# Attention products in 64-row tiles with the rounded part above the remainder, and new work lists, in a gated S4D and Infini-attention kernel

## The chip, the cores and the metric

The kernel runs on one core of a Trainium2 chip. Its time is the device time of one execution in microseconds (us); before the change three runs took 835.3, 832.37 and 835.19 us, median 835.19. PE is TensorE (the matrix engine), PEld its weight loads, DVE is VectorE, ACT is ScalarE, POOL is GpSimd, SP is SyncE, which here only issues transfers. Transfers are issued from SP's, ACT's and POOL's queues, each in order.

## What is computed

The input u has 2048 rows of 448 values. Two mixers work on it, and a gate per row joins them:

```python
g = sigmoid((u * gate_w).sum(-1))
out = g * A(u) + (1 - g) * B(u)
```

A is a long convolution along the rows: for each of 448 channels a kernel K of length 2048 is a sum over 256 complex exponentials, and y = irfft(rfft(u) * rfft(K)) + u * D_skip, with transforms of length 4096.

B is attention with memory: q, k and v are projections of u (16 heads of 28), the rows are cut into 4 segments of 512. In each segment and head:

```python
p = softmax(q @ k.T * scale + causal_mask)
o = sig(beta) * (phi(q) @ M) / (phi(q) @ z) + (1 - sig(beta)) * (p @ v)
M, z = M + phi(k).T @ v, z + phi(k).sum(0)
```

and the result is o @ wo. A softmax subtracts the largest logit of each row before the exponential.

## The kernel before

The program has two halves, one after the other on the same engines.

The first half builds the convolution kernel K. `first_half` (line 256 on) goes through 56 steps n: PE makes arguments (`turns`), ACT takes sines and cosines of them (`trig`), DVE multiplies them with decays (`product`), PE sums the products (`sums`), and POOL scales. Between these, at 190 places called slots, other work is fed in: `project` computes q, k, v, the memory and the gate, and `transform_u` the first Fourier step of u. The list FEED says how many steps of `project` go into each slot, FILL how many of `transform_u`, VECTOR at which slots the copies out of PSUM run on DVE instead of ACT, and UNREAD how many products without use (`k.turn_over`, 128 columns of bf16) stand ahead of each `sums`. The engines keep the order in which the program writes this. q and k are stored to DRAM (QD, KD) in two parts: `hi`, rounded to the type fp32r, and `lo`, the remainder. A weights' matrix, its rounded part and its remainder are treated likewise; `project` reads 128 rows of u at a time into `xin`, columns 384 to 447 twice (lines 922 and 923), since the last block of 64 columns is to fill 128.

The second half does the rest. `second_half` reads a list of words, PROGRAM, letter by letter; each letter issues one step:

- K: one of 8 steps of `transform_k`, the first Fourier step of K over its 64 x 112 sums; two PSUM tiles are copied out, one by ACT, one by DVE, and stored (GK).
- l: `load(i)`, q and k of the next of 16 units (a unit is one segment and 4 heads).
- A: one of 6 steps of `maxima(i)`: logits of two heads on PE, row maxima on DVE. The logits use the rounded parts alone.
- B: the end of a unit's maxima: a transpose, the negative maxima rounded and their remainder (`mn`), and a write of them into row 28 of q, from POOL's queue (line 1075). Since k has 1 in its row 28 and q and k have 28 values a head, the next product already gives the logit less the maximum.
- W: one of 6 steps of `weigh(i)`: transposed logits of two heads on PE, in three products (hi by hi, lo by hi, hi by lo), then the exponential on ACT; a seventh W issues POOL's masks. P is two W steps of one kind abreast.
- V: the weights times v. E: the end of a segment (division by the sums, the memory's part, the output projection).
- C: a step of `convolve`: second Fourier step of K and u in 64-row tiles, their product on POOL, the way back; its loads run three steps ahead. F, b, j, z: the last step of the convolution and the join with the gate. G, w, S, D: the gate, wo, the skip term, a division of the last segment.
- t: a product without use, 128 rows, 512 columns, bf16 (`turn_over`).

A head has 28 values in a tile of 32 rows, so four heads fill 128 partitions, and the products of A and W are issued in tiles of 32 rows of the array: A works on heads 2 and 3 where W works on heads 0 and 1, and the other way round (`MSTEPS`, line 1038). `PLACES` lists the blocks below the diagonal: 512 columns, then 384 and 128, then 256.

The tiles of q and k have 4 buffers each. Space and order of the transfers: `k.dma` issues from SP and is kept behind the last marked transfer (`k.mark`).

## Time and profile before

| | |
|---|---|
| runs (us) | 835.3, 832.37, 835.19 |
| the profiled execution, by the same clock (us) | 836.45 |
| its span in the trace (us) | 834.7 |
| busy: PE, DVE, ACT, POOL (us) | 727.2, 569.5, 555.2, 239.1 |
| granted PE clock, mean | 0.950 |
| moved by DMA | 153.99 MB, 184 GB/s on average |

The span is cut below at 66, 85, 436, 490 and 740 us from its start. Up to about 66 us the parameters are prepared, up to 436 us the loop of the first half runs, then the passage, in which the K steps and the first units stand, and from about 490 us attention and convolution go side by side; after 740 us the convolution's last step and the last segment remain. Busy times of PE count matmuls from issue to the modelled end of the pipeline, so they overlap and are no measure of throughput. "Granted clock" is the share of full speed that the throttle gave to PE.

### The profile page before, as it was taken

To read this page: it belongs to the slowest core of one execution; us is meant where nothing else is said; L and a number is where in the kernel's file an instruction comes from. 1 tells how busy PE (TensorE), PEld (TensorE's weight loads), DVE (VectorE), ACT (ScalarE), POOL (GpSimd) and SP (SyncE) were. 2 spreads that over 40 slices of the span, in tenths; PEclk is the share of its full clock that TensorE was granted. 3 is DMA by queue.
4 is the path that set the end of the run, shared out by engine and by line. 5 is a ranking of instruction groups with operands and counts; after the bars stand their busy time and mean duration, and the time that the engine had idled before them with its cause. 6 is when DMAs were issued, how large, how long until landed. Compare 5 with 4: busy or idle time off the path is not lost.

```text
span 834.7 us, 19015 instructions
## 1 busy us (share of the span) xinstructions
PE 727.2 (87%) x7557; PEld 398.3 (48%) x7582; DVE 569.5 (68%) x1134; ACT 555.2 (67%) x663; POOL 239.1 (29%) x249
## 2 busy tenths in 40 slices
PE   1576998999879999799979899999999899988977
PEld 1353555665546655456644454444444344444433
DVE  7969489857989579886785864544554545666773
ACT  3767789979999899988872266765466544641320
POOL 4404210111001111011110035564545545752210
PEclk9879999999999999999995889999999899999999
DMA  8527775145552455513647877685466565556775
GB/s 206 157 60 241 226 241 175 59 137 181 176 169 66 137 177 178 170 54 135 201 150 295 306 238 219 196 269 172 171 215 215 156 233 175 194 185 253 216 227 150
DMA packets 91987, 153.99 MB, mean 184 GB/s; under 512 B 23106, under 2 KB 60346, under 8 KB 91850
## 3 DMA queue, kind: packets, MB, share of 16 engines
q1 hardware_dynamic: 82826, 141.70, 53.2%
q10 hardware_dynamic: 7424, 9.18, 3.2%
q0 software_dynamic: 1648, 1.89, 0.8%
q8 instruction: 60, 0.98, 0.5%
q14 instruction: 29, 0.24, 0.1%
HBM read 91.74 MB, written 60.63 MB: 183 GB/s over the span
## 4 chain that ended last, share of the span: by engine, by line
PE 45%; DVE 18%; ACT 16%; DMA 9%; issue 7%; POOL 2%; SPq 1%; ACTq 0%; DVEq 0%; POOLq 0%
PE ps_m L1429 19%; PE ps_a L1429 18%; ACT cs L1394 7%; DVE Y L399 4%; DVE jk L1063 4%; PE ps_arg L1429 3%; PE ps_k L1429 3%; DVE X L395 2%; DVE Y L400 2%; ACT L1394 2%; PE ps_m L1432 1%; DMA r<-RD 1%; ACT EX L1394 1%; DMA bt<-BB 1%; DMA ce<-in_c_ce 1%
## 5 line engine op out<-in xcount | busy, mean ns | idle before, releaser
L1063 DVE CUSTOM_DVE_ANT_0 jk<-ps_a,mk 128x512 f32<-128x512 f32 (+3 forms) x256 | 125.1, 489 | 77.7 <-PE ps_a L1429 69.6
L361 POOL TENSOR_TENSOR EX<-EX,cab 128x1024 f32<-128x1024 f32 x28 | 53.5, 1913 | 301.7 <-ACT EX L1394 277.5
L1099 ACT ACTIVATE PT<-ps_a 128x1024 f32<-128x1024 f32 (+1 forms) x96 | 83.0, 880 | 69.6 <-PE ps_a L1429 68.6
L1394 ACT ACTIVATE cs<-ps_arg 128x1024 f32<-128x1024 f32 x111 | 107.4, 1023 | 1.4 <-DVE Y L400 0.8
L1429 PE MATMUL ps_a<-qu,ku 32*128 32x384 f32 (+3 forms) x768 | 78.3, 351 | 5.9 <-DVE mx L1063 5.0
L1429 PE MATMUL ps_m<-xh,w 128*128 128x512 f32 x224 | 81.8, 417 | 1.7 <-DMA w<-WD 1.4
L395 DVE TENSOR_TENSOR X<-EX,cs 128x1024 f32<-128x1024 f32 x56 | 69.2, 1236 | 17.8 <-ACT cs L1394 17.6
L663 POOL TENSOR_TENSOR pr<-us,ks 128x896 f32<-128x896 f32 x32 | 67.1, 2095 | 30.2 <-ACT us L662 30.1
L1110 POOL TENSOR_SCALAR_AFFINE_SELECT PT<-PT 128x256 f32<-128x256 f32 (+1 forms) x96 | 48.2, 507 | 93.3 <-ACT PT L1099 91.7
L1429 PE MATMUL ps_k<-Y,X 128*32 128x64 f32 x3584 | 62.2, 221 | 14.3 <-DVE Y L400 14.0
L1429 PEld LDWEIGHTS ps_k<-Y,X 128*32 128x32 f32 x3584 | 52.9, 110 | 39.1 <-DVE Y L400 27.0
L399 DVE TENSOR_TENSOR Y<-EY,cs 128x1024 f32<-128x1024 f32 x56 | 70.0, 1251 | 0.0
L1429 PEld LDWEIGHTS ps_a<-qu,ku 32*128 32x128 f32 x768 | 55.3, 193 | 20.2 <-DVE mx L1063 9.7
L1394 ACT ACTIVATE EY<-ps_arg 128x1024 f32<-128x1024 f32 x52 | 53.0, 1034 | 17.8 <-PE ps_arg L1429 16.4
L1394 ACT ACTIVATE cs<-cs 128x1024 f32<-128x1024 f32 x56 | 59.3, 1059 | 1.8
L401 DVE SCALAR_TENSOR_TENSOR Y<-EY,cs 128x512 f32<-128x512 f32 x56 | 40.9, 732 | 27.9 <-ACT cs L1394 25.8
L1429 PEld LDWEIGHTS ps_m<-xh,w 128*128 128x128 f32 x224 | 42.0, 187 | 21.9 <-issue 7.9
L1429 PE MATMUL ps_a<-ku,qu 32*128 32x512 f32 (+3 forms) x256 | 47.4, 404 | 4.5 <-DVE mx L1063 1.7
L1429 PE MATMUL ps_arg<-ct,lh 64*128 64x512 bf16 x224 | 45.5, 380 | 6.0 <-ACT cs L1394 4.3
L1429 PE MATMUL ps_m<-xl,w 128*128 128x512 f32 x128 | 50.2, 393 | 0.0
L1429 PEld LDWEIGHTS <-lh 64*128 64x128 bf16 x392 | 22.9, 95 | 55.2 <-issue 41.7
L1429 PEld LDWEIGHTS ps_a<-ku,qu 32*128 32x128 f32 x256 | 23.1, 195 | 48.2 <-issue 21.8
(215 smaller groups left out, 1429.4 us busy)
## 6 DMA issues: line engine op xcount, KB each, us to landing
w<-WD SPq DMA_DIRECT2D x32, 448.0 KB, 4.5
qu<-QD SPq DMA_DIRECT2D x16, 512.0 KB, 4.0
ku<-KD SPq DMA_DIRECT2D x16, 512.0 KB, 5.1
GU<-gs SPq DMA_DIRECT2D x32, 224.0 KB, 2.4
GK<-gs SPq DMA_DIRECT2D x8, 896.0 KB, 4.7
gk<-GK SPq DMA_DIRECT2D x32, 224.0 KB, 3.8
gu<-GU SPq DMA_DIRECT2D x32, 224.0 KB, 2.5
BB<-bs ACTq DMA_DIRECT2D x16, 448.0 KB, 4.5
```

Of the source, the lines that this page charges most:

```text
L361: nc.gpsimd.tensor_tensor(o, o, cab, ALU.mult)
L395: v.tensor_tensor(X, ex, t[:, :, 0], ALU.mult)
L399: v.tensor_tensor(Y[:, :, :, :32], lo, y[:, :, :, ::-1], ALU.mult)
L400: v.tensor_tensor(Y[:, 0, :, 32:], ey[:, :, 32:], y[:, 0], ALU.mult)
L401: v.scalar_tensor_tensor(Y[:, 1, :, 32:], ey[:, :, 32:], -1.0, y[:, 1], ALU.mult, ALU.mult)
L663: nc.gpsimd.tensor_tensor(pr[c], us, ks.pop(c), ALU.mult)
L1063: v.tensor_tensor_reduce(junk[:, :n], pt[:, x, o : o + n], k.mk[:, SEG - n :], 1.0, -3e38, ALU.add, ALU.max, mx[:, 3 - t, h : h + 1],)
L1099: nc.scalar.activation(PT[:, 2 * hp : 2 * hp + 2, 512 * b : 512 * b + n], pt[:, :, :n], AF.Exp, scale=SCALE)
L1110: nc.gpsimd.affine_select(sl, sl, pat, ALU.is_ge, 0.0, base=0, channel_multiplier=-1)
L1394: x = op(*args, **kw)
L1429: tc.keep_in_program_order(nc.tensor.matmul(*args, **kw))
L1432: tc.keep_in_program_order(nc.tensor.transpose(*args))
```

## The change

1. **q and k in 64-row tiles.** A unit's q now lies with heads in two row halves of 64: in each, 32 rows of the rounded part above 32 rows of the remainder; the other two heads lie beside them in a free dimension. k lies in the same rows twice, over both parts. One product over 64 rows then gives hi and lo of q at once against hi of k, and a second one against lo of k: two products where there were three (the product of the two remainders comes in as well). A's logits use both parts of q against hi of k, in one product as before. Both A and W use all 128 rows for two heads. P and `k.abreast` are gone, and each W step is on its own.
2. **Loads.** Eight transfers a unit instead of two, with k's bytes loaded twice; three buffers instead of four for q and for k. Unit 0's go over POOL's queue. The first two tiles of weights and the first of v are placed before the loads. The write of the negative maxima is four transfers instead of one, `mn` has one buffer instead of two, and `gs` of `transform_k` three instead of four.
3. **First half.** The second read of u's last columns becomes a copy on POOL; gate_w is loaded over POOL's queue. FEED, UNREAD, VECTOR and FILL have new numbers: UNREAD's sum goes from 24 to 94, VECTOR's from 66 to 78, FILL's from 9 to 10; FEED's stays 249.
4. **Words.** A new PROGRAM: t goes from 141 to 196 letters, a new letter T (two products without use in the two 64-row tiles) stands 17 times, P (9) is gone and W goes from 94 to 112; one K step (k) has both copies on ACT.

```diff
@@ -459,21 +459,21 @@
 FEED = (
-    2, 0, 3, 0, 1, 0, 2, 0, 1, 3, 8, 0, 0,
...
+    2, 0, 3, 0, 1, 0, 3, 0, 0, 3, 8, 0, 0,
...
@@ -491,30 +491,30 @@
 UNREAD = (
...
-    0, 0, 0, 0, 0, 0, 0, 0, 0, 0, 0, 16, 0, 8,
+    0, 0, 0, 0, 0, 0, 0, 0, 0, 8, 0, 0, 0, 0,
+    0, 0, 0, 16, 0, 0, 0, 0, 0, 0, 0, 4, 0, 0,
+    0, 0, 0, 0, 0, 0, 4, 0, 0, 0, 0, 0, 0, 20,
+    8, 0, 0, 0, 0, 0, 0, 2, 0, 0, 0, 16, 8, 8,
 )
...
@@ -600,7 +600,7 @@
     for i in range(8):
-        gs = fp.tile([128, 4, 4, 112], F32, tag="gs", name="gs", bufs=4)
+        gs = fp.tile([128, 4, 4, 112], F32, tag="gs", name="gs", bufs=3)
@@ -613,7 +613,7 @@
             pt = pts[jj][:, :, :448].rearrange("p j (n q) -> p j n q", n=4)
-            if jj == 0:
+            if jj == 0 or k.scalar_only:
@@ -739,9 +739,9 @@
     nc.gpsimd.memset(gw, 0.0)
-    nc.sync.dma_start(gw[:, :3, 0], k.gate_w[:384].rearrange("(k p) -> p k", p=128))
+    k.pdma(gw[:, :3, 0], k.gate_w[:384].rearrange("(k p) -> p k", p=128))
     for h in range(2):
-        nc.sync.dma_start(gw[64 * h : 64 * h + 64, 3, 0], k.gate_w[384:])
+        k.pdma(gw[64 * h : 64 * h + 64, 3, 0], k.gate_w[384:])
@@ -920,7 +920,7 @@
                 nc.sync.dma_start(xin[:, :D], k.u[rs])
-                nc.sync.dma_start(xin[:, D:], k.u[rs, 384:])
+            nc.gpsimd.tensor_copy(xin[:, D:], xin[:, 384:D])
@@ -1019,16 +1019,31 @@
     Q, K, W, Vs, pvss = {}, {}, {}, {}, {}
+
+    def weights_tile():
+        return ap.tile([128, 4, 1280], F32, tag="PT", name="PT", bufs=2)
+
+    def values_tile():
+        return ap.tile([128, 4, SEG], F32, tag="V", name="V", bufs=1)
+
+    W[0], W[1], Vs[0] = weights_tile(), weights_tile(), values_tile()
     last = {}
 
     def load(i):
         if i >= 16:
             return
         s, hg = divmod(i, 4)
-        for t, T, src in (("q", Q, k.QD), ("k", K, k.KD)):
-            T[i] = ap.tile([128, 2, SEG], F32R, tag=t, name=t + "u", bufs=4)
-            x = k.dma(T[i].bitcast(F32), src[s, hg])
-        if i < 3:
+        Q[i] = ap.tile([128, 2, SEG], F32R, tag="q", name="qu", bufs=3)
+        K[i] = ap.tile([128, 2, 2, SEG], F32R, tag="k", name="ku", bufs=3)
+        qd = k.QD[s, hg].rearrange("(p j e) b q -> j b e p q", p=2, j=2)
+        kd = k.KD[s, hg].rearrange("(p j e) b q -> j e p b q", p=2, j=2)
+        for j in range(2):
+            for b in range(2):
+                r = slice(64 * j + 32 * b, 64 * j + 32 * b + 32)
+                queue = k.dma if i else k.pdma
+                queue(Q[i][r].bitcast(F32), qd[j, b])
+                x = queue(K[i][r].bitcast(F32), kd[j])
+        if 0 < i < 3:
@@ -1050,15 +1065,14 @@
                 for x in range(2):
-                    h = 2 * hp + x
-                    r = slice(32 * h, 32 * h + 32)
+                    r = slice(64 * x, 64 * x + 64)
                     k.mm(
-                        pt[:, x, o : o + n], q[r, 0, 128 * qt : 128 * qt + 128], kk[r, 0, :n],
-                        start=True, stop=True, tile_position=(32 * h, 0),
+                        pt[:, x, o : o + n], q[r, hp, 128 * qt : 128 * qt + 128], kk[r, hp, 0, :n],
+                        start=True, stop=True, tile_position=(64 * x, 0),
                     )
             for t, o, n in PLACES[b]:
                 for x in range(2):
-                    h = 2 * hp + x
+                    h = 2 * x + hp
@@ -1069,36 +1083,35 @@
             k.tr(pm[:4, 128 * qt : 128 * qt + 128], mx[:, qt], k.ident)
-        mn = ap.tile([4, 2, SEG], F32R, tag="mn", name="mn", bufs=2)
+        mn = ap.tile([4, 2, SEG], F32R, tag="mn", name="mn", bufs=1)
         nc.scalar.activation(mn[:, 0], pm[:4], AF.Copy, scale=-1.0)
         v.scalar_tensor_tensor(mn[:, 1], pm[:4], -1.0, mn[:, 0], ALU.mult, ALU.subtract)
-        k.pdma(q.rearrange("(j e) i q -> e j i q", e=32)[28].bitcast(F32), mn.bitcast(F32))
+        for b in range(2):
+            for j in range(2):
+                r = 64 * j + 32 * b + 28
+                k.pdma(q[r : r + 1].bitcast(F32), mn[2 * j : 2 * j + 2, b].bitcast(F32))
         yield
 
     def weigh(i):
 
         q, kk = Q.pop(i), K.pop(i)
-        W[i] = PT = ap.tile([128, 4, 1280], F32, tag="PT", name="PT", bufs=2)
-        steps = list(STEPS)
-        while steps:
-            now = [steps.pop(0) for _ in range(k.abreast)]
-            pts = [k.ps("a") for _ in now]
-            b = now[0][0]
+        if i not in W:
+            W[i] = weights_tile()
+        PT = W[i]
+        for b, hp in STEPS:
+            pt = k.ps("a")
             for kt, o, n in PLACES[b]:
-                for a, (x, y) in enumerate(((0, 0), (1, 0), (0, 1))):
-                    for (_, hp), pt in zip(now, pts):
-                        for z in range(2):
-                            h = 2 * hp + z
-                            r = slice(32 * h, 32 * h + 32)
-                            k.mm(
-                                pt[:, z, o : o + n], kk[r, x, 128 * kt : 128 * kt + 128], q[r, y, 128 * kt :],
-                                start=(a == 0), stop=(a == 2), tile_position=(32 * h, 0),
-                            )
+                for a in range(2):
+                    for z in range(2):
+                        r = slice(64 * z, 64 * z + 64)
+                        k.mm(
+                            pt[:, z, o : o + n], kk[r, hp, a, 128 * kt : 128 * kt + 128], q[r, hp, 128 * kt :],
+                            start=(a == 0), stop=(a == 1), tile_position=(64 * z, 0),
+                        )
             n = 512 if b < 2 else 256
-            for (_, hp), pt in zip(now, pts):
-                nc.scalar.activation(
-                    PT[:, 2 * hp : 2 * hp + 2, 512 * b : 512 * b + n], pt[:, :, :n], AF.Exp, scale=SCALE
-                )
+            nc.scalar.activation(
+                PT[:, 2 * hp : 2 * hp + 2, 512 * b : 512 * b + n], pt[:, :, :n], AF.Exp, scale=SCALE
+            )
@@ -1112,7 +1125,8 @@
         if hg == 0:
-            Vs[s] = ap.tile([128, 4, SEG], F32, tag="V", name="V", bufs=1)
+            if s not in Vs:
+                Vs[s] = values_tile()
@@ -1292,6 +1306,20 @@
 
+    k.scalar_only = False
+
+    def first_step():
+        k.scalar_only = True
+        next(first)
+        k.scalar_only = False
+
+    def turn_halves(n):
+        pt = k.ps("a")
+        for _ in range(n):
+            for h in range(2):
+                r = slice(64 * h, 64 * h + 64)
+                k.mm(pt[:, h], wz[r, :128], wz[r], start=True, stop=True, tile_position=(64 * h, 0))
+
@@ -1314,13 +1342,6 @@
         k.load_b, k.join, k.final = finish(nc, k, fin())
-
-    k.abreast = 1
-
-    def both():
-        k.abreast = 2
-        next(weights)
-        k.abreast = 1
@@ -1333,10 +1354,10 @@
         "K": lambda: next(first),
+        "k": first_step,
         "G": gates,
         "C": lambda: next(k.cv),
         "W": lambda: next(weights),
-        "P": both,
@@ -1349,6 +1370,9 @@
                 continue
+            if c == "T":
+                turn_halves(n)
+                continue
@@ -1359,23 +1383,23 @@
 PROGRAM = """
-KlAKAAlKAKKAAtAKKBAKtVGCttAtttAtttAttt
-AAWAtWAlBtWWAtttAWtttAWW
-lAVPtCABCAWCtAWCtttWACWtttACWwAV
-lWtCCAWVBCAWCtCtAWtttWACtttAWCWV
-ABPlCAVCCAWCAWCtttAWCtttAWCWV
-lAWCAWVBCAWECCtCAWEEtttVWEWACtttAWCAl
-WEWAVCBCAWECCtAWECtttAWECtttAWECWV
-lAWECAWVBCAECtAPECCtttAWECtttAWECWlAV
-ECAPVBCAWCtAWCtttAWCCtttAWCWV
-ACAtPVBClAECAttWWtECttttEWAECCtttVAWW
-ltCAWECAWVBCAWECtAWECttWAECtttACWECWV
-lAWEAWCVBCECAWtAWECtttAWEttCtAWECWV
-lAECCAWWVBCAWCStAWCAWtCtttttttWAtWCV
-AWtClCAWVBCACtAtECPCEtEEttttACtttAWWF
-VbWWABAbEAWEVttEEWEEbtAWEbbttVEWtttttAEEWtttttEAWjWjjjjj
-WVBzDtbtWjWztjbWztbVDWzW
-zPVzzttPDzPtVtW
+KKlAkAtttltAAtAtKAttKKKttttttttttttVTTTTTKAttBttAttGtTTTCTAAtttA
+tttttttWTTTTAtttAABtAtttttttWAttttWttAttWtWAWWl
+tCttWWVBCCAWtAtAWttVCWtAWtAtWCCtAClw
+WtCWVBCAWtCAWttCAWttCVAtCAAttttWWWl
+WCCVBCWCAttttAtWAtCACtWtWAtWttAl
+WCCVWVBCAWtECCtAWEEEtttCAWAtttttAWWVttttCAl
+tCWCCEWWVBACECAWECttAWAEtCttAtWAECW
+ECWlWVBCEACWtAWECVCAV
+WtEWAWtltWCEACAECWCVBCAWWtAWCAWttCAWtCtAWlA
+ttVCtWVBCAECEtEAtWCWCtWAttCAVCCWAtEtWlt
+tWAWtCCEVBWACEAWCECtWAECWWtttAVEtCAl
+tCAEWWVBCECAWtAtWAECtttAWECAEVtWCWA
+ElCCWWVBCAWStCAWCAtWttCAttAWtWttAltV
+WtCCWCWVBCAEttttAEECCWttCAWtWtAECtttttWAtVFbTTTTAttttBtltAE
+WEbVttAEWWEEEAtttbAWEAEbAWEbttWttttttEEjjjVjjW
+WjtVBWDztjbtWWzztbWWjDbzWVzW
+WVWzzWDWWVttzWt
```

57 rows, old and new, of tables (FEED, FILL, UNREAD, VECTOR) are left out of this document.

## The prediction

> **What bounds the kernel now.** I read the page first, for the span and the clock.
>
> ```profile
> span 834.7 us, 19015 instructions
> PE 727.2 (87%) x7557; PEld 398.3 (48%) x7582; DVE 569.5 (68%) x1134; ACT 555.2 (67%) x663; POOL 239.1 (29%) x249
> PEclk9879999999999999999995889999999899999999
> ```
>
> The last row is the granted clock in 40 slices, in tenths; it is lowest just past the middle. So I cut the span at the places where the work changes and asked for busy times by stretch (columns: PE, weight loads, DVE, ACT, POOL, granted clock, DMA share, GB/s).
>
> ```profile
> 0.00:66.00 66.00, 32.47 (x123) 21.83 (x125) 50.86 (x80) 40.09 (x55) 21.06 (x30) 0.84 0.54 143
> 85.00:436.00 351.00, 318.90 (x4730) 200.88 (x4732) 275.80 (x389) 312.52 (x362) 52.52 (x29) 0.99 0.48 155
> 436.00:490.00 54.00, 47.83 (x305) 25.01 (x300) 35.15 (x110) 13.69 (x16) 5.58 (x9) 0.68 0.81 294
> 490.00:740.00 250.00, 237.38 (x1710) 108.31 (x1718) 130.15 (x437) 149.80 (x181) 131.60 (x145) 0.98 0.63 200
> 740.00:834.70 94.70, 79.05 (x487) 36.65 (x488) 58.85 (x106) 23.43 (x32) 20.07 (x32) 0.95 0.65 204
> ```
>
> Five stages with five limits. Up to 66 us it is the parameter chain: DVE 50.9 of 66. From 85 to 436 us (the S4D kernel with the projections threaded through it) PE, ACT and DVE are 91%, 89% and 79% busy and hand each other work; none is full. From 436 to 490 us, the passage between the halves, PE is busy at a clock of 0.68, with the DMA at 294 GB/s. From 490 to 740 us (attention beside the convolution) PE is 95% busy and sets the pace. The tail is waits.
>
> **Fewer products.** A weigh step (W) now issues three products for two heads in 32-row tiles, a maxima step (A) one product for the other two heads. The third W product goes: 256 of 768 instructions in these groups.
>
> ```profile
> L1429 PE MATMUL ps_a<-qu,ku 32*128 32x512 f32 x192 | 26.8, 440 | 3.2 <-DVE mx L1063 3.2
> L1429 PE MATMUL ps_a<-qu,ku 32*128 32x256 f32 x192 | 19.7, 323 | 1.3 <-DVE mx L1063 1.3
> ```
>
> A third of such busy time would suggest a gain of some 20 us. But these are pipelined durations, so I looked at starts. First an A step beside a W step, then a W step alone, then an A step alone, all 256 wide, each with what follows; then the same pair 512 wide.
>
> ```profile
> 500.62 0.39 PE L1429 MATMUL ps_a<-qu,ku 32*128 32x256 f32 x2
> 500.64 0.38 PE L1429 MATMUL ps_a<-ku,qu 32*128 32x256 f32 x2
> 500.84 0.40 PE L1429 MATMUL ps_a<-qu,ku 32*128 32x256 f32 x4
> 501.17 1.02 PE L1429 MATMUL ps_a<-gu,cf 64*128 64x448 f32 x4
> 502.12 0.62 PE L1429 MATMUL ps_a<-qu,ku 32*128 32x256 f32 x6
> 502.67 0.82 PE L1429 MATMUL ps_m<-wz 128*128 128x512 bf16 x3
> 503.42 0.38 PE L1429 MATMUL ps_a<-ku,qu 32*128 32x256 f32 x2
> 503.74 0.65 PE L1429 MATMUL ps_a<-gk,cf 64*128 64x448 f32 x2
> ...
> 508.62 0.50 PE L1429 MATMUL ps_a<-ku,qu 32*128 32x512 f32 x2
> 508.63 0.96 PE L1429 MATMUL ps_a<-qu,ku 32*128 32x512 f32 x6
> 509.52 0.64 PE L1429 MATMUL ps_m<-PT,V 128*32 128x512 f32 x4
> ```
>
> A and W together take 0.55 us (500.62 to 501.17), W alone takes 0.55 (502.12 to 502.67): the A step is free, because it works in the 64 rows of the array that W leaves empty (MSTEPS swaps the head pairs for just this). A alone costs 0.32. With 64-row tiles both steps fill the array, and that cover is gone: A's one round and W's two come to the three rounds of today. **Where A stands next to W the edit gains nothing.**
>
> The rest by rounds (one round is one product of two heads): (0.55 - 0.32) / 2 = 0.115 us at 256 columns, so about 0.23 at 512 and at 384 + 128, on average 0.2. There are 96 W steps; 18 of them are run as nine pairs (P), two abreast in the four row groups. 78 single steps lose a round: 78 x 0.2 = -15.6 us. The nine P go from three rounds to four: +1.8. Following the starts as above, 48 of 96 A steps run under a W (the word list has 51 neighbours AW); they surface: +9.6. Net **-4 us**, not -20. Bounds: 0, if P and hidden A take it all back, and -16, if the surfaced A steps fall into waits.
>
> By the Trainium skill ("TensorEngine Tiling (Array Packing)", Key Properties) a change of tiling mode drains the engine, and the new tiles have the mode of the gk and gu products, so borders would get cheaper. At 503.42 an A step followed by gk takes 0.2 us more than a round; if half of that were drain, some 60 borders would give an estimated -6 us more. No row here shows a border without a change of mode, so I take nothing for it.
>
> **The passage.** K steps (the Fourier steps of the S4D kernel) run here. Two of them by time, and the stretches by 4 us:
>
> ```profile
> 437.79 3.37 PE L1429 MATMUL ps_a<-kb,s1k 32*128 32x448 f32 x16 [1.25 <-DVE kb L422]
> 467.22 2.22 PE L1429 MATMUL ps_a<-kb,s1k 32*128 32x448 f32 x16
> 442.15 0.79 PE L1429 MATMUL ps_a<-ku,qu 32*128 32x512 f32 x2 [0.98 <-DMA ku<-KD]
> 442.16 1.53 PE L1429 MATMUL ps_a<-kb,s1k 32*128 32x448 f32 x4
> ...
> 450.00:454.00 4.00, 4.00 (x24) 1.93 (x20) 2.45 (x9) 0.92 (x1) 0.00 (x0) 0.50 1.00 395
> 454.00:458.00 4.00, 4.00 (x30) 2.32 (x22) 1.70 (x7) 1.05 (x2) 0.00 (x0) 0.59 0.51 208
> 470.00:474.00 4.00, 3.98 (x23) 1.64 (x21) 3.64 (x14) 0.00 (x0) 0.00 (x0) 1.00 0.94 305
> 478.00:482.00 4.00, 3.59 (x17) 2.18 (x19) 3.15 (x12) 1.56 (x2) 0.70 (x2) 0.50 1.02 402
> ```
>
> The same 16 instructions take 3.37 us at clock 0.5 and 2.22 at 1.0. Between 450 and 458 PE is never idle and the clock stays near half; between 470 and 474, where full-height filler products (wz) run, it is 1.0. I read this as: half-filled rows don't raise the clock, dense fillers do. The new words put 57 t (one full-height filler) and 13 T (two 64-row fillers) into their first two lines, where 21 t stood. The stage's clock of 0.68 means 0.64 x 54 = 34 us at half; if all of it were bound by PE, full clock would give back 17 us. But bytes set a floor: 294 GB/s x 54 us = 15.9 MB, plus 1.5 MB more for three units (below), at the best stretch's 402 GB/s is 43 us, so at most 11 us can go. The added fillers cost (57 + 13 - 21) x about 0.2 = 10 us where nothing else waits. I take half of the cap: **-6 us** (from -11 to +6).
>
> The Trainium skill ("TensorE: Matmul & The Clock Gate", Why this matters for your kernels) asks only that TensorE be kept busy for 4 us continuously to get full clock. The rows of 450 to 458 differ: 8 us busy at about half. By that rule the fillers would add nothing where PE is busy already, and my estimate for the passage would be 0 instead of -6, 829 us in all.
>
> Unit 0's eight transfers go to POOL's queue, and the tiles W[0], W[1] and Vs[0] are placed first. Today A waits 0.98 us for ku (442.15, above), landing after SP had stood behind the last transfers of the first half. That is -1 us, in the 6.
>
> **More transfers.** Issues, with KB each and time to landing, and the queue time of the row-28 write:
>
> ```profile
> qu<-QD SPq DMA_DIRECT2D x16, 512.0 KB, 4.0
> ku<-KD SPq DMA_DIRECT2D x16, 512.0 KB, 5.1
> ...
> 502.78 0.32 SPq L1445 DMA_DIRECT2D qu<-QD  x1
> 503.15 0.42 SPq L1445 DMA_DIRECT2D ku<-KD  x1
> ...
> L1075 POOL DMA_DIRECT2D qu<-mn x16 | 9.6, 602 | 56.0 <-DVE mn L1074 54.5 <-DVE mx L1063 1.5
> ```
>
> K goes to both row halves: 1024 KB instead of 512 a unit, 8 MB in all; at 0.63 DMA share from 490 us on there is room. Each unit issues eight transfers instead of two: six more at 0.37 us on SP, 2.2 us, with the convolution's loads queued behind them; these are fetched three steps ahead. The maxima's write becomes four issues: 3 x 0.6 = 1.8 us more on POOL for each unit, 29 us in all, in front of the products and selects there. POOL is 53% busy from 490 on, so it fits on average; where it comes between a maxima and the weigh step that needs it, it shows: up to 1.8 us x 16 = 29, at least 0. I take +2.
>
> With three buffers instead of four, load n waits for unit n-3's weighing, and the words put it only about ten letters ahead of its first A (unit 7: "tCWCCEWWVB"), where some 34 letters stood. Landing takes about 5.1 + 2.2 + 0.5 MB at 200 to 400 GB/s (1.3 to 2.5) = 9 to 10 us. The ten letters hold three C (1.02 of PE each, from the gu row), three W (about 0.5) and a V, a B and an E, for which I allow 1 to 2 us each: 8 to 11 us. That is a tie; I take +2 for it, bounds 0 and +26 (2 us for 13 units).
>
> Against that, 490 to 740 us has clock 0.98, so 10 us at half; full clock gives at most -5. Of the 72 t and T more than now, the 23 outside the passage are +5 if nothing covers them. These two go out even. So steady state: -4 + 2 + 2 = **0 us**, and the tail, with one unit's weighing less, -1.
>
> **The first half.** Twelve more slots put their copies on DVE.
>
> ```profile
> L1394 ACT ACTIVATE gs<-ps_m 128x448 f32<-128x448 f32 x18 | 9.7, 537 | 1.4 <-PE ps_m L1429 1.4
> L1394 DVE COPY gs<-ps_m 128x448 f32<-128x448 f32 x14 | 8.5, 619 | 2.7 <-PE ps_m L1429 2.2 <-DMA GU<-gs 0.4
> 428.82 0.90 PE L1429 MATMUL ps_k<-ct,one 128*128 128x128 bf16 x13
> 12.25 0.58 SPq L922 DMA_DIRECT2D xin<-in_A_u  x1
> 12.91 0.40 SPq L923 DMA_DIRECT2D xin<-in_A_u  x1
> ```
>
> That is 12 x 0.54 = 6 us off ACT, the busier, and 12 x 0.62 = 7 onto DVE, which has 75 us free. 70 more small fillers (UNREAD 24 to 94) at 0.90 / 13 = 0.07 us are 5 us of PE ahead of sums that wait for DVE, against 7 us at half clock (0.99 of 351), worth 3.5. FEED moves steps between slots and keeps 249. Nothing sizes that; by 7 us either way. 16 small xin transfers (0.40 us of SP) become POOL copies, cheap but behind POOL's parameter work at the start; gate_w's three leave SP. With all this I take **-4 us** (-9 to +6) for the loop, -1 for the start.
>
> Two smaller buffers cost nothing: a K store lands in about 5 us while two more stand in gs, and mn's single buffer is asked for again only a unit later, some 15 us; without that cover each would add its landing, about 5 us, a time.
>
> Sum: -1 - 4 - 6 + 0 - 1 = -12 on the profiled execution's 836.45 us (span 834.7), so 824.5. That execution stands 1.3 us above the median of the runs, 835.19; against the median I forecast **823 us**.
>
> **The rivals.** About 4.2 us, 0.5%, is what a measurement can tell from no change: 831 to 839.4.
>
> - Nothing gained (chance 0.14): the passage is held by its bytes (+6) and the surfaced A steps take back all that W saves (+4): -12 + 6 + 4 = -2, 833 us. For it: the 0.55 beside 0.55, and 395 to 402 GB/s. Against: clock 0.50 with PE busy.
> - Late loads, slower (0.15): the tie between load and first A is lost. What stands behind a waiting A on PE waits too, as the K products at 442.16 did; here that is W, C and fillers, and behind them ACT and V. At 2 us for each of 13 units, +24 beyond the 2 taken: +12, 847 us. It decides from about 1.1 us a unit. For it: three buffers, eight issues, ten letters; against: the words hold fillers just there that can be waiting time anyway.
> - Bigger gain (0.17): the passage gets its 11, the surfaced A steps lie in waits, the loop gets 9: -12 - 5 - 5 - 5 = -27, 808 us.
> - The clock in the passage doesn't rise (0.07): 829 us; the fillers don't do what I read into the rows.
> - My forecast (0.47), 813 to 831 us.
>
> Faster 0.47 + 0.17 + 0.07 = 0.71; same 0.14; slower 0.15. The range of 8 in 10 reaches from 808 into the no-change case and stops short of most of the late loads: 808 to 838 us.
>
> **What would show it.** In the changed profile: 512 weigh products, and no A step beginning with a W step; a W at 256 columns of about 0.43 us alone. Clock of the passage above 0.85, and its length between 43 and 50 us. POOL's row-28 write 64 issues. A steps whose wait names ku are the late loads; a PE share from 490 us on under 0.9 with such waits would make the forecast wrong, as would a passage at clock 0.7, or a loop longer than 351 us.

## The result: slower by 4%

The changed kernel takes 866.32 us (median of 4 runs, 864.1 to 874.76) where the kernel before took 834.07 beside it (4 runs, 832.37 to 835.3). The ratio is 1.0407, 95% interval 1.0332 to 1.0482. The forecast was 823 us. The ratios here and below compare the means of each kernel's executions that lie within 1.5% of its fastest, while the times in us are medians of all of them. The profiled execution after took 864.1 us, 27.7 more than the one of before (836.45).

The page of the changed kernel: span, busy times and granted clock, then from the chain of waits the line by tiles.

```profile
span 862.4 us, 19146 instructions
PE 754.0 (87%) x7485; PEld 410.0 (48%) x7485; DVE 579.1 (67%) x1136; ACT 551.8 (64%) x661; POOL 273.0 (32%) x324
PEclk9788999999989999999998999999899996898989
...
PE ps_m L1453 22%; PE ps_a L1453 15%; DMA ku<-KD 5%; ACT cs L1418 4%; PE ps_arg L1453 4%; PE ps_k L1453 4%; DVE Y L399 4%; DVE X L395 3%; DVE Y L400 2%; SPq L1469 2%; DVE jk L1077 2%; PE ps_m L1456 1%; ACT L1418 1%; DMA w<-WD 1%; DVE Y L401 1%
```

The load of k (ku) stands third in the chain, with 5% of the span.

To see where the time went I took three landmarks that both kernels have: the last `sums` of the first half, ACT's copy of the values of unit 0, and its copy of those of unit 13. Timeline rows (start and length in us, then the instruction), first of the kernel before, then of the changed one:

```profile
435.44 1.10 PE L1429 MATMUL ps_k<-Y,X 128*32 128x64 f32 x64 [2.00 <-DVE Y L400]
491.33 0.60 ACT L1130 ACTIVATE pvs<-ps_m 128x512 f32<-128x512 f32 x1 [1.95 <-PE ps_m L1429]
780.58 0.60 ACT L1130 ACTIVATE pvs<-ps_m 128x512 f32<-128x512 f32 x1 [0.33 <-PE ps_m L1429]
```

```profile
426.57 1.10 PE L1453 MATMUL ps_k<-Y,X 128*32 128x64 f32 x64 [1.82 <-DVE Y L400]
493.14 0.60 ACT L1144 ACTIVATE pvs<-ps_m 128x512 f32<-128x512 f32 x1 [0.79 <-PE ps_m L1453]
807.71 0.60 ACT L1144 ACTIVATE pvs<-ps_m 128x512 f32<-128x512 f32 x1 [1.76 <-PE ps_m L1453]
```

By the ends of these rows (start plus length):

| stage (us) | before | after | difference | forecast |
|---|---|---|---|---|
| start to the last `sums` | 436.5 | 427.7 | -8.9 | -5 |
| passage, to unit 0's values | 55.4 | 66.1 | +10.7 | -6 |
| thirteen units, to unit 13's values | 289.2 | 314.6 | +25.3 | 0 |
| tail, to the end of the span | 53.5 | 54.1 | +0.6 | -1 |

The first half gained more than I had said. The second half lost 36.6 us. How it works now, by stretches (columns: length, busy PE, weight loads, DVE, ACT, POOL, granted clock, DMA share, GB/s):

```profile
85.00:436.00 351.00, 322.62 (x4838) 204.65 (x4837) 283.48 (x393) 311.66 (x359) 61.37 (x49) 0.99 0.50 158
436.00:490.00 54.00, 45.39 (x277) 20.12 (x275) 30.63 (x105) 13.51 (x16) 6.96 (x14) 0.94 0.86 266
490.00:740.00 250.00, 226.20 (x1414) 106.01 (x1410) 121.76 (x381) 134.66 (x167) 136.29 (x165) 0.95 0.76 205
```

From 490 to 740 us PE's busy time fell from 237.4 to 226.2 us: it waits more. The DMA share rose from 0.63 to 0.76, though the throughput hardly did (200 to 205 GB/s). So the engines of the DMA need nearly a fifth more time for a byte, over all transfers (0.76 / 205 against 0.63 / 200). The clock of the passage is 0.94 instead of 0.68, as the forecast wanted, and yet the passage is longer. The groups and issues that the change touches:

```profile
L1453 PE MATMUL ps_a<-ku,qu 64*128 64x512 f32 (+3 forms) x256 | 52.7, 426 | 21.4 <-DMA ku<-KD 11.6
L1453 PE MATMUL ps_a<-qu,ku 64*128 64x256 f32 (+3 forms) x512 | 65.8, 359 | 4.3 <-DVE mx L1077 2.6
L1092 POOL DMA_DIRECT2D qu<-mn x64 | 32.6, 515 | 58.9 <-ACT mn L1087 58.3
```
```profile
ku<-KD SPq DMA_DIRECT2D x60, 256.0 KB, 6.0
qu<-QD SPq DMA_DIRECT2D x60, 128.0 KB, 4.7
```

The products and writes are as counted: 512 weigh products, 64 writes of the maxima. But the maxima's products (first row) wait for k. One of these waits, on PE's timeline, is unit 5's; above it, the first and the last of the eight issues of that unit's loads on SP:

```profile
527.14 0.32 SPq L1469 DMA_DIRECT2D qu<-QD  x1
...
530.48 0.43 SPq L1469 DMA_DIRECT2D ku<-KD  x1
```

```profile
534.65 0.54 PE L1453 MATMUL ps_a<-ku,qu 64*128 64x512 f32 x1
537.50 0.47 PE L1453 MATMUL ps_a<-ku,qu 64*128 64x512 f32 x1 [2.31 <-DMA ku<-KD]
537.90 0.79 PE L1453 MATMUL ps_m<-wz 128*128 128x512 bf16 x2
```

The first product, on rows 0 to 63, has its data; the second, on rows 64 to 127, starts 2.8 us later. Everything behind it on PE waits with it. The same pair is apart by 2.8 to 3.2 us at 494.8, 554.0, 669.8 and 771.0 us. These are units 3, 5, 6, 11 and 15. Their leads (the time from the first issue of a unit's loads to its first A product) are 6.9, 7.5, 6.9, 8.4 and 7.9 us. The other units loaded from SP's queue have leads of 10.4 us or more and no such wait. From a unit's first issue to its last packet of k the median is 9.6 us (units 3 to 15).

### The profile page after: what moved, and what is told of

It reads as the page before. It is cut to its first block, busy times and chain, and to the rows that moved or that the text cites. A ratio compares the mean times of both kernels' runs of the same rounds, so it can differ in the third digit from the quotient of the medians.

```text
span 862.4 us, 19146 instructions
## 1 busy us (share of the span) xinstructions
PE 754.0 (87%) x7485; PEld 410.0 (48%) x7485; DVE 579.1 (67%) x1136; ACT 551.8 (64%) x661; POOL 273.0 (32%) x324
## 4 chain that ended last, share of the span: by engine, by line
PE 47%; DVE 15%; DMA 13%; issue 10%; ACT 10%; SPq 2%; POOL 2%; ACTq 0%; DVEq 0%; POOLq 0%
PE ps_m L1453 22%; PE ps_a L1453 15%; DMA ku<-KD 5%; ACT cs L1418 4%; PE ps_arg L1453 4%; PE ps_k L1453 4%; DVE Y L399 4%; DVE X L395 3%; DVE Y L400 2%; SPq L1469 2%; DVE jk L1077 2%; PE ps_m L1456 1%; ACT L1418 1%; DMA w<-WD 1%; DVE Y L401 1%
## 5 line engine op out<-in xcount | busy, mean ns | idle before, releaser
L395 DVE TENSOR_TENSOR X<-EX,cs 128x1024 f32<-128x1024 f32 x56 | 71.1, 1270 | 13.9 <-ACT cs L1418 13.8
L1453 PE MATMUL ps_a<-ku,qu 64*128 64x512 f32 (+3 forms) x256 | 52.7, 426 | 21.4 <-DMA ku<-KD 11.6
L1453 PE MATMUL ps_a<-qu,ku 64*128 64x256 f32 (+3 forms) x512 | 65.8, 359 | 4.3 <-DVE mx L1077 2.6
L1453 PEld LDWEIGHTS ps_k<-Y,X 128*32 128x32 f32 x3584 | 54.1, 112 | 29.6 <-DVE Y L400 17.9
L1453 PE MATMUL ps_m<-wz 128*128 128x512 bf16 x196 | 61.8, 398 | 0.2
L401 DVE SCALAR_TENSOR_TENSOR Y<-EY,cs 128x512 f32<-128x512 f32 x56 | 43.5, 779 | 25.0 <-ACT cs L1418 22.2
L1453 PEld LDWEIGHTS ps_a<-qu,ku 64*128 64x128 f32 x512 | 44.9, 194 | 28.3 <-issue 11.6
L1453 PEld LDWEIGHTS ps_a<-ku,qu 64*128 64x128 f32 x256 | 24.5, 193 | 58.1 <-issue 32.2
L1088 DVE SCALAR_TENSOR_TENSOR mn<-ps_m,mn 4x512 fp32r<-4x512 f32 x16 | 10.8, 677 | 60.2 <-ACT mn L1087 60.2
L1092 POOL DMA_DIRECT2D qu<-mn x64 | 32.6, 515 | 58.9 <-ACT mn L1087 58.3
```

Of the source, the lines that this page charges most:

```text
L395: v.tensor_tensor(X, ex, t[:, :, 0], ALU.mult)
L401: v.scalar_tensor_tensor(Y[:, 1, :, 32:], ey[:, :, 32:], -1.0, y[:, 1], ALU.mult, ALU.mult)
L1092: k.pdma(q[r : r + 1].bitcast(F32), mn[2 * j : 2 * j + 2, b].bitcast(F32))
L1453: tc.keep_in_program_order(nc.tensor.matmul(*args, **kw))
```

## The experiments

### Which part loses: the first half alone, and whole-height loads

e1: the kernel before with the first half's part of the change only (new FEED, FILL, UNREAD, VECTOR; the copy on POOL; gate_w over POOL).

```diff
-                nc.sync.dma_start(xin[:, D:], k.u[rs, 384:])
+            nc.gpsimd.tensor_copy(xin[:, D:], xin[:, 384:D])
...
```

> The kernel before with the change's first half alone (FEED, FILL, UNREAD, VECTOR, the copy on POOL for the second read of u, gate_w over POOL). In the two traces the last sum of the first half ends at 436.5 us before and at 427.7 us after. Theory A, the first half's edits are a gain and all of the loss lies in the second half: last sum at 426 to 430 us and a time of about 834 - 9 = 825 us. Rival B, the early end only pulls forward work that the second half's transfers or PE then wait for: 832 to 836 us.

829.83 us (822.95 to 835.03, 10 runs), ratio 0.9948 (0.9908 to 0.9989). The first half's part gains 4.3 us by the ratio, which lies between the two expectations. The changed kernel's loss is in the second half's part.

e2: the changed kernel, with each unit's loads as two transfers over all 128 rows. The bytes are as many, but come from other places of QD and KD, so the logits are computed from other values.

```diff
-                queue(Q[i][r].bitcast(F32), qd[j, b])
-                x = queue(K[i][r].bitcast(F32), kd[j])
+        queue(Q[i].bitcast(F32), k.QD[s, hg])
...
+        x = queue(K[i].rearrange("r p a q -> r (p a) q").bitcast(F32), kd)
```

> The changed kernel, with q and k of each unit loaded in one transfer of 128 rows each, the same bytes but read from other places of QD and KD, so logits are computed from wrong values; only the transfers' shape and number differ. Theory A, the loss comes from transfers to 32 rows that land late: the packets of 4096 bytes go from some 306 ns back to some 180, A steps no longer wait for ku (10 us in four waits between 504 and 803 us), the passage loses some 6 us, so 866 - 16 = 850 us or less. Rival B, the words cost it (fillers, A steps without a W beside them, what stands behind them): packets get faster, but the time stays at 860 to 868 us.

836.8 us (828.44 to 847.14, 10 runs), ratio 1.0023 (0.9987 to 1.006): some 30 us of loss are gone. Its landmarks, and the same place on PE as above:

```profile
426.25 1.10 PE L1450 MATMUL ps_k<-Y,X 128*32 128x64 f32 x64 [1.82 <-DVE Y L400]
485.54 0.60 ACT L1141 ACTIVATE pvs<-ps_m 128x512 f32<-128x512 f32 x1 [0.79 <-PE ps_m L1450]
779.91 0.60 ACT L1141 ACTIVATE pvs<-ps_m 128x512 f32<-128x512 f32 x1 [1.76 <-PE ps_m L1450]
...
523.01 0.51 PE L1450 MATMUL ps_a<-ku,qu 64*128 64x512 f32 x2
523.44 1.04 PE L1450 MATMUL ps_m<-wz 128*128 128x512 bf16 x4
```

The two products start together. Beside the changed kernel the passage is 7.3 us shorter and the thirteen units 20.2. The waits of PE for ku fall from 11.6 us to 0.7, which is 10.9 of the 20.2. Another 7.4 are busy time of PE (287.0 us in the changed kernel's thirteen units, 279.5 here, at granted clocks of 0.94 and 0.96); why the clock is lower with the late loads isn't shown.

The leads of e2 are nearly the same (6.9 to 13.9 us in units 3 to 11), but the last packet of k comes 6.4 us after the first issue (median of units 3 to 15). And e2 is not as fast as e1: by the ratios it stands 0.75% or some 6 us above it. So the rest of the second half's part loses time too, without the narrow loads.

### What about the loads: their number, their order, their queue, their height

e9 keeps eight transfers of the same sizes, but each over all 128 rows (again from other places). e3 is the kernel before with each load cut into four of 32 rows. e12 alternates the two row halves on the queue, e11 issues the lower half from ACT's queue.

```diff
+        for c in range(4):                                    # e9, in place of the loop over j and b
+            h = slice(256 * (c % 2), 256 * (c % 2) + 256)
+            queue(Q[i][:, c // 2, h].bitcast(F32), k.QD[s, hg, :, c // 2, h])
+            x = queue(kt[:, c].bitcast(F32), kd[:, c])
```
```diff
-            x = k.dma(T[i].bitcast(F32), src[s, hg])          # e3
+            for j in range(4):
+                r = slice(32 * j, 32 * j + 32)
+                x = k.dma(T[i][r].bitcast(F32), src[s, hg, r])
```
```diff
-        for j in range(2):                                    # e12
-            for b in range(2):
+        for b in range(2):
+            for j in range(2):
-                queue = k.dma if i else k.pdma                # e11
+                queue = (k.adma if j else k.dma) if i else k.pdma
```

> The changed kernel with eight transfers a unit as it has them, but each to all 128 rows (q in four parts of 256 columns, k in four of 512), the same bytes, again read from other places, so the logits are from wrong values. With two such transfers the time was 836.8 us. Theory A, what costs the 30 us is the 32 rows of each transfer, not their number: 837 to 842 us, no packet of 2048 bytes of k much above 100 ns. Rival B, the number of issues on SP's queue (six more a unit) costs as much: 850 us or more.

> The kernel before, with each of its loads of q and k cut into four transfers of 32 rows; bytes, buffers and words as before. Theory A, narrow transfers are slower by the packet but the lead of 15 to 33 us between a load and its first A step covers them: packets of 4096 bytes in the second half at some 300 ns, time at 834 to 840 us, the few us in the passage. Rival B, narrow transfers cost time by themselves, whatever the lead, since the convolution's loads stand behind them: 845 us or more. Rival C, the packets don't get slower by it: the slow packets of the changed kernel have another cause.

> The changed kernel with its eight loads of a unit in another order on the same queue: rows 0 to 31, 64 to 95, 32 to 63, 96 to 127, so that transfers that follow each other go to different halves. Theory A, the engines run ahead of each other enough to mix the halves: packets of 4096 bytes below 290 ns and 850 to 860 us. Rival B, they stay in step: 862 to 868 us.

> The changed kernel with the transfers to rows 64 to 127 issued from ACT's queue and those to rows 0 to 63 from SP's, so that both row halves can be written at one time; shape, number and bytes as in the change. Theory A, the 32-row transfers are slow because all 16 DMA engines write to the same 32 rows at a time: with two halves in flight the 4096-byte packets fall below 306 ns and the time to 845 to 858 us. Rival B (the Trainium skill, 'SBUF — State Buffer', Can I just issue two DMAs to hit both halves?, has +6% at most): packets and time stay, 860 to 868 us.

| run | us | ratio | interval |
|---|---|---|---|
| e9, eight transfers of 128 rows | 839.33 | 0.9979 | 0.9923 to 1.0035 |
| e3, before with 32-row loads | 842.25 | 1.013 | 1.0074 to 1.0186 |
| e12, halves in turn | 865.62 | 1.0396 | 1.027 to 1.0522 |
| e11, halves on two queues | 868.84 | 1.0378 | 1.027 to 1.0486 |

Eight transfers of 128 rows (e9) cost between nothing, by the ratio, and 5.0 us, by the medians (839.33 against 834.31 before), where the changed kernel loses 32. Transfers of 32 rows cost the old kernel 1.3% with the old bytes and four buffers (e3), between the two expectations. So it is in the main the height, not the number. The DMA issues of e9, to be held beside those of the changed kernel above, with the same sizes and counts (the last figure is the median of the few issues whose landing the profile shows):

```profile
ku<-KD SPq DMA_DIRECT2D x60, 256.0 KB, 4.9
qu<-QD SPq DMA_DIRECT2D x60, 128.0 KB, 4.5
```

In the DMA records of 490 to 740 us, the packets of 4096 bytes on SP's queue have a median of 159 ns before (128 rows), 326 ns after (32 rows), and 253 in e3; the means are 184, 306 and 254. The other loads on that queue come later too: over the whole span the convolution's gk and gu land in 5.5 and 6.6 us after, 3.8 and 2.5 before (3.4 and 5.0 in e9). The Trainium skill ("SBUF — State Buffer", Door 1: The DMA port swizzle) says that a transfer reaches 16 ports only with rows of both halves of the 128, and that 32 or 64 neighbouring rows of one half reach 8, half the rate. The two-fold median agrees; the mean (1.7 times) and e3 (1.4 to 1.6 times) stay below it. In e11 the mean packet fell from 306 ns to 254 on SP's queue and 267 on ACT's, in e12 to 291, and the time did not fall by anything that these intervals of 1% to either side can tell. In e11 the waits for ku fell as well, from 11.6 us to 6.1. The same page ("Can I just issue two DMAs to hit both halves?") gives two transfers on the two halves only 6% over one; the packets of e11 gain 13 to 17% here, but the kernel shows no gain.

### The new layout in DRAM, for whole-height loads

e10: q and k are stored in DRAM in the order in which they are loaded (k twice, rows of the two parts in turn), so that plain 128-row loads carry the right values. The price is 128 stores of 64 rows in the first half.

```diff
-            nc.sync.dma_start(dst[s, hg, :, i], x.bitcast(F32))
+            for p in range(2):
+                xr = x[64 * p : 64 * p + 64].bitcast(F32)
+                if nm == 0:
+                    nc.sync.dma_start(k.QD[s, hg].rearrange("(r b) p q -> b p r q", b=2)[i, p], xr)
...
```

> The changed kernel with the right values and plain loads: the rows of the rounded part and of the remainder alternate (row 64 j + 2 e + b), and the first half stores q and k to DRAM in that order, k twice, in stores of 64 rows (128 stores where 64 stood); each unit then loads q and k in one transfer of 128 rows each. Theory A: the loads were the loss, so 835 to 843 us, near the 837 of the plain loads from wrong places, with 0 to 6 us for the stores. Rival B: the stores, of 64 rows each and with twice the bytes of k, hold up SP's queue in the first half, and the loss comes back there: 850 us or more, with the last sum of the first half after 440 us.

846.67 us (840.97 to 855.67, 4 runs), ratio 1.012 (1.0022 to 1.0218). With right values the whole-height loads are worth 19.7 us against the changed kernel; against the kernel before they are still no gain. The last `sums` ends at 440.4 us instead of 427.7: the stores cost some 12 us of the first half, and so take back part of what the loads save in the second. The time lies between the two expectations.

### How much is the lead, how much the bytes

The forecast said that the words put a load "only about ten letters ahead of its first A". e13 tests this with the 32-row loads of e3: from unit 3 on, each l is moved to ten letters before the unit's first A.

```diff
-AAWAtWAlBtWWAtttAWtttAWW
-lAVPtCABCAWCtAWCtttWACWtttACWwAV
...
+WAtWABtWWAtlttAWtttAWWAVPtCABCAWCtAWCttt
...
```

> The kernel before with its loads cut into transfers of 32 rows (842 us, 1.013 of before) and in its words each load from unit 3 on moved to ten letters ahead of the unit's first A, as near as the changed kernel has it; four buffers, two products hidden, and k loaded once, as before. Theory A, narrow transfers and a short lead together make the loss, so most of the changed kernel's 25 us from unit 0 to unit 13 come up here too: 855 to 865 us, with A steps waiting for ku. Rival B, the lead matters little while a unit has 1 MB and not 1.5 MB: 840 to 847 us.

841.9 us (836.73 to 849.5, 4 runs), ratio 1.016 (1.0071 to 1.0248), the same as e3. It didn't test the lead: in units 3 to 15 that is 17 to 33 us, and 19 to 33 in e3. With four buffers, a load goes out when the last W of the unit four back ends (0.03 us after it in most units of both runs), wherever its letter stands up to there. So it is the buffers that set the lead. In the changed kernel, with three, the first issue of units 3 to 11 follows that W by under 0.2 us, and the first A comes 6.9 to 13.9 us after it.

e14 leaves k's remainder out: the rounded part stands in both products, a unit's loads are 1.0 MB instead of 1.5, in pieces of 32 rows, with three buffers. e15 is the same with four buffers, for which that leaves room.

```diff
-        K[i] = ap.tile([128, 2, 2, SEG], F32R, tag="k", name="ku", bufs=3)
+        K[i] = ap.tile([128, 2, 1, SEG], F32R, tag="k", name="ku", bufs=3)     # e15: bufs=4, q too
...
```

> The changed kernel with k's remainder left out: the rounded part alone is loaded (into both row halves) and stands in both products of the weigh step, so the output lacks the remainder's part. A unit's loads fall from 1.5 to 1.0 MB, still in pieces of 32 rows; three buffers as in the change. Theory A (the short lead that three buffers leave is what the loads run out of): the time barely falls, 850 to 862 us. Theory B (bytes at the half rate): 1.0 MB at the half rate lasts as long as 1.5 MB would at two thirds of full rate, and the time falls to 838 to 846 us. Neither: above 862 us.

> The run before with four buffers for q and k instead of three (there is room for them only because k's remainder is left out), so that each load goes out one unit earlier. Theory A (lead): 836 to 845 us, 10 us or more below the run before. Theory B (bytes at the half rate): no further fall, within 4 us of the run before.

e14: 834.56 us (829.38 to 842.42, 10 runs), ratio 0.9992 (0.995 to 1.0034). e15: 827.38 (822.9 to 830.89, 10 runs), 0.9898 (0.9851 to 0.9945). Landmarks of e14, its unit 5 (its first load issued at 519.48 us), and its issues of k; then the landmarks of e15:

```profile
489.61 0.60 ACT L1144 ACTIVATE pvs<-ps_m 128x512 f32<-128x512 f32 x1 [0.84 <-PE ps_m L1453]
782.46 0.60 ACT L1144 ACTIVATE pvs<-ps_m 128x512 f32<-128x512 f32 x1 [1.76 <-PE ps_m L1453]
...
526.99 0.68 PE L1453 MATMUL ps_a<-ku,qu 64*128 64x512 f32 x2
```
```profile
ku<-KD SPq DMA_DIRECT2D x60, 128.0 KB, 3.5
```

```profile
489.53 0.60 ACT L1144 ACTIVATE pvs<-ps_m 128x512 f32<-128x512 f32 x1 [0.79 <-PE ps_m L1453]
773.67 0.60 ACT L1144 ACTIVATE pvs<-ps_m 128x512 f32<-128x512 f32 x1 [1.76 <-PE ps_m L1453]
```

Unit 5's lead is 7.5 us in e14 (519.48 to 526.99) as in the changed kernel (527.14 to 534.65), and now both products of the pair start together; an issue of k lands in 3.5 us instead of 6.0. Half a megabyte less takes 21.7 us off the thirteen units (314.6 to 292.9); the fourth buffer takes off 8.7 more (to 284.1). Both times miss the ranges: e14 is faster than either theory said, and e15's further fall lies between them. Neither theory had it alone: the bytes of narrow loads are the larger part, the short lead is worth 0.9% on top, and with whole-height loads or fewer bytes three buffers already suffice for the kernel to be as fast as before. The packets of k are 2048 bytes in e14 and 4096 in the changed kernel, so fewer bytes and smaller packets aren't separated.

### The terms of the sum, one by one

e4: the kernel before without W's third product (hi of k by lo of q), the rest as it was; the remainder of q is missing from the logits. e7: the kernel before, with A on the same rows as W, so that A loses its cover. e8: the write of the maxima in four transfers. e6: e2 without the t and T from the third word line on (139 t, 4 T).

```diff
-                for a, (x, y) in enumerate(((0, 0), (1, 0), (0, 1))):     # e4
+                for a, (x, y) in enumerate(((0, 0), (1, 0))):
-    MSTEPS = [(b, 1 - hp) for b, hp in STEPS]                             # e7
+    MSTEPS = STEPS
-        k.pdma(q.rearrange("(j e) i q -> e j i q", e=32)[28].bitcast(F32), mn.bitcast(F32))   # e8
+        for j in range(4):
+            r = 32 * j + 28
+            k.pdma(q[r : r + 1].bitcast(F32), mn[j : j + 1].bitcast(F32))
-tCttWWVBCCAWtAtAWttVCWtAWtAtWCCtAClw                                  # e6, and so on
+CWWVBCCAWAAWVCWAWAWCCAClw
...
```

> The kernel before, with the third product of each weigh step (hi of k by lo of q) left out, so the logits lack that part; tiles of 32 rows, words and loads as before, and A steps still run beside W steps. It gives the price of the product with the cover kept. Theory A (the rounds of the prediction): 78 single steps and 9 pairs lose a round of 0.2 us, -17 us, so about 817 us. Rival B, PE's rounds in the second half stand beside other waits: -5 us or less, 829 to 834 us.

> The kernel before with maxima steps in the same head order as the weigh steps (MSTEPS = STEPS), so that an A next to a W works in the same rows of the array and is no longer under it; the results are the same. It prices the cover that the 64-row tiles give up. Theory A (the prediction): 48 A steps surface at 0.2 us, +9.6, so about 844 us. Rival B, PE finds the time in waits: 834 to 838 us.

> The kernel before with the write of the negative maxima cut in four, one for each head, on POOL's queue. Theory A (the prediction): 1.8 us more of POOL for each unit, +2 us, 834 to 838. Rival B, the masks and products queued behind it on POOL hold PE: up to 29 us, 845 to 863 us.

> The kernel with two plain 128-row loads a unit (836.8 us, wrong values of the logits), without the 139 t and 4 T from the third line of the words on. Theory A, these fillers stand in waits or keep the clock, so their going gains little or loses: 834 to 845 us. Rival B, they hold PE up: up to 143 x 0.2 = 28 us faster, 810 to 825 us.

| run | us | ratio | interval | term in the forecast |
|---|---|---|---|---|
| e4, two products | 828.46 | 0.9927 | 0.9893 to 0.9961 | -15.6 (-17 with the nine pairs) |
| e7, no cover for A | 838.0 | 1.0052 | 1.0017 to 1.0086 | +9.6 |
| e8, four writes | 833.44 | 1.0012 | 0.9973 to 1.005 | +2 |
| e6, without late fillers | 837.02 | 1.0056 | 1.0022 to 1.0089 | +5 for the 23 added |

In us of 834.3, W's third round is worth 6.1 and A's cover 4.3; the writes cost nothing that can be measured; the late fillers, all 143 of them, cost nothing net (e6 is as slow as e2). Of W and A the signs were right, the sizes two to three times too large. That the rounds lie in part in time in which PE waits anyway would explain this, and the rivals of e4 and e7 said so, but no run shows it.

### The passage

e16 is e2 with only the old number of fillers, 21 t, in the first two word lines. e17 is e1 with 58 t there instead of 21.

```diff
-KKlAkAtttltAAtAtKAttKKKttttttttttttVTTTTTKAttBttAttGtTTTCTAAtttA          # e16
+KKlAkAtlAAtAKAtKKKtttVKAtBAtGtCAAtA
...
-KlAKAAlKAKKAAtAKKBAKtVGCttAtttAtttAttt                                    # e17
+KlAKAAttlKAttKKAAtttAKtttKtttBAKttttttVtttGtttCtttAttttAttttttAttttttt
...
```

> Run e2 (the changed kernel with whole-height loads from wrong places) with the fillers of the passage cut back to what the kernel before had: 21 t in the first two word lines in place of 57 t and 13 T. Forecast's reading (the fillers raise the clock and this shortens the passage by 6 us): the passage's clock falls to about 0.7 and the time rises by some 6 us over e2, to 841 to 845. Rival (the fillers take as long as the clock gives back): the clock falls and the time stays within 3 us of e2, 834 to 840. Second rival (they cost more than the clock gives): 826 to 833.

> Run e1 (the kernel before with the first half's part of the change, the best so far) with 58 t in the first two word lines in place of 21. Forecast's reading: clock of the passage from 0.83 to above 0.9 and some 4 to 6 us less than e1, 822 to 826. Rival (cost and gain cancel): 827 to 833. Second rival (37 fillers at about 0.2 us come on top): 834 to 840.

e16: 834.91 us (831.97 to 837.85, 10 runs), ratio 0.9996 (0.9972 to 1.0019), beside 1.0023 for e2: no difference that can be told. e17: 824.43 us (822.52 to 826.9, 4 runs), ratio 0.9864 (0.9831 to 0.9897), faster than both kernels; e1 has 0.9948 (0.9908 to 0.9989), beside other runs of the kernel before. The stated reading of the forecast had 822 to 826 us for e17 and some 4 to 6 us less than e1; the medians differ by 5.4. The stretch between the halves of e2, e16, e1 and e17, in this order (columns as above):

```profile
428.00:480.00 52.00, 47.25 (x300) 21.07 (x300) 32.37 (x104) 13.72 (x16) 6.52 (x13) 0.97 0.77 284
```
```profile
428.00:480.00 52.00, 39.78 (x271) 18.77 (x276) 31.29 (x99) 11.37 (x13) 6.45 (x11) 0.80 0.76 272
```
```profile
428.00:479.00 51.00, 45.62 (x301) 22.07 (x301) 35.47 (x112) 14.49 (x18) 5.17 (x9) 0.83 0.89 331
```
```profile
428.00:479.00 51.00, 44.79 (x360) 21.71 (x369) 35.86 (x116) 13.57 (x16) 5.66 (x9) 0.97 0.86 317
```

In both pairs the fillers raise the clock, from 0.80 to 0.97 and from 0.83 to 0.97. The profiled executions show no shorter passage: from the last `sums` to unit 0's values it is 58.8 us in e2 and 60.4 in e16, and 51.1 in e1 and 51.6 in e17. The two pairs disagree in their runs. e16 is as fast as e2, which is the rival's case. e17 is faster than e1 as the forecast's reading said, with intervals that don't overlap, and the traces can't tell where: the profiled execution is the fastest of e1's ten (822.95 us) and the slowest of e17's four (826.9). One execution also says little of a few us in a stage: e8, as fast as the kernel before, has 294.0 us in the thirteen units and 47.4 in the tail, where that has 289.2 and 53.5.

Why the changed passage is the longest, 66.1 us, the waits for gs show. Rows of the waits over the whole span of the changed kernel, then of e2 (who waits, for what: us, times, longest); the waits for ku all lie behind the passage, which ends at 493.7 us in the one and 486.1 in the other:

```profile
PE ps_a L1453 <- DMA ku<-KD: 11.6, 5, 2.7
ACT gs L617 <- DMA GK<-gs: 10.6, 2, 9.1
DVE gs L619 <- DMA GK<-gs: 8.5, 1, 8.5
```
```profile
PE ps_a L1450 <- DMA ku<-KD: 0.7, 1, 0.7
ACT gs L617 <- DMA GK<-gs: 2.4, 1, 2.4
DVE gs L619 <- DMA GK<-gs: 1.6, 1, 1.6
```

The K steps' copies wait up to 9.1 us for a stored gs to leave its buffer. With whole-height loads they wait 2.4. The copy that waits longest starts at 460.76 us, and its fellow in e2 at 453.33: 7.4 us, as much as the passages differ. The narrow loads of units 1 and 2 are issued in that stretch (436.6 to 451.0 us), on the queue of these stores. In e3, with narrow loads and four gs buffers, no wait of a copy is put down to a store of GK (one of 3.6 us is put down to ku), and the passage is 56.7 us. What remains of e2's passage over the old one (58.8 to 55.4 us, and to 51.1 in e1) isn't settled: it isn't the fillers (e16), and the order of the words, the third gs buffer and the wait for the four writes weren't separated.

## Why the prediction was wrong

- **The step that failed is "More transfers", and in it the tie between landing and lead.** The landing, 9 to 10 us, was right as a number: the median from first issue to last packet of k is 9.6 us. That is in part luck, for it was put together from landings of transfers over 128 rows, and with two such transfers e2 has 6.4. The lead, 8 to 11 us, was right only in the middle: in units 3 to 11 it runs from 6.9 to 13.9. A tie in the mean is a loss in each unit that lies under it, and PE waits for ku in just the five units with less than 9.6. And the price of +2 had nothing for the rows that a load goes to: with 32 rows a packet of 4096 bytes takes the DMA engines 1.7 times the time in the mean (306 against 184 ns). Measured: +25.3 us over thirteen units, 1.9 a unit, of which e2 gives back 20.2. That is the rival "late loads", held at 0.15, with its price of 2 us a unit, and its point of decision (1.1 us) was passed. The sign named for it came as well: A steps whose wait names ku. The stated range, which ended at 838 us, left it out.
- **The evidence was at hand.** The same issues are 512 KB to 128 rows before; afterwards each goes to 32. The prediction counted issues and bytes, and asked nowhere to how many rows they go. "At 0.63 DMA share from 490 us on there is room" held in the mean, for the share is 0.76 after, and helped nothing: what counts is how long one unit's loads take against its lead.
- **"Two smaller buffers cost nothing" failed for gs.** The cover it named, two more stores in gs, holds only while a store lands in about 5 us; here a copy waited 9.1 us. With whole-height loads and the same three buffers (e2) it waited 2.4, and 7.3 us of the passage come back. So it is the narrow loads beside the third buffer, and not the third buffer alone.
- **The passage's -6** failed as well: +10.7, and e2 has still +3.4. The rows on half-filled tiles and the clock were read rightly: the clock of the passage rose to 0.94, and to 0.97 in e2 and e17, and in e17 with PE no busier than in e1 (44.8 against 45.6 of 51 us). By the Trainium skill ("TensorE: Matmul & The Clock Gate", Why this matters for your kernels) the fillers should have added no clock where PE is busy already; the rows of e17 and e1 disagree. In e2 PE is also busier than in e16 (47.3 against 39.8 of 52 us), so that pair doesn't decide it. But in the profiled executions the clock wasn't what bounded the passage: e2 at 0.97 and e16 at 0.80 take nearly the same time there, and so do e17 and e1. Only the runs of e17 speak for the -6. The first rival's "held by its bytes" fits the passages better, but no run here shows it by itself.
- **The first half's -5** (start and loop) was right in sign: -8.9 in the trace, -4.3 over the runs of e1. The 1 us for unit 0's transfers can't be told from it.
- **W and A.** "Where A stands next to W the edit gains nothing" is borne out in the 32-row tiles: the third product is worth 6.1 us and the cover 4.3, so some -2 where I had -4, if the two add up. A W step of 256 columns takes about 0.4 us after (median of 32, from its first start to the next product), near the "about 0.43".
- **The second half without the narrow loads.** Passage, W and A, writes and tail were to give -9; e2 stands 6 us above e1 instead. In the profiled executions its passage is 7.7 us longer than in e1, its thirteen units also 7.7 (294.4 against 286.7) and its tail 4.1 shorter. Why fewer products don't show in the thirteen units stays open.
- **The small terms.** Four writes: 0 instead of +2. Late fillers: 0 net (e6) where the 23 added were +5, and the -5 for a fuller clock from 490 us on didn't come either (0.95 after, 0.98 before).

In sum, against 824.5 us on the profiled execution: -3.9 in the first half, +16.7 in the passage, +25.3 in the thirteen units, +1.6 in the tail, 39.7 us in all, which makes the 864.1 measured.

## What to carry to other kernels

Before a layout is changed, ask of every transfer how many of the 128 rows it goes to, not only how many bytes it has: here a packet to 32 rows took the DMA engines 1.4 to 1.7 times the mean time of one to 128, and the loads cost several times what a third of the weigh products was worth. A load's lead is set by when its buffer comes free; take the time from the last reader of that buffer to the first reader of the new data, from the trace, and not the place of its issue in the program. Take it unit by unit: a tie in the mean is lost in every unit that lies below it. A low clock or a busy engine in a stretch is worth its share only if nothing else ends that stretch at the same time.

## What was not expected of the hardware

- A load of 32 rows needs a median of 326 ns (mean 306) for a packet of 4096 bytes where one of 128 rows needs 159 (mean 184); sending the two row halves from two queues brings the mean to 254 and 267 ns, and the kernel no gain that can be told.
- PE's granted clock goes from 0.80 or 0.83 to 0.97 when dense products without use are put between products of 32 and 64 rows, in a stretch whose length stays the same within 2 us.
- Executions of one kernel lie up to 1.7% apart (829.64 to 843.35 us in 19 runs of the kernel before), so that a term of 2 us can be told only over many runs.
